# Attention row sums: from the exponentials' accumulator to adds of halves on GpSimd and a sum of 16 columns on VectorE

## The chip, the cores and the metric

The kernel runs on one core of a Trainium2 chip. The metric is the time of one execution on the device in microseconds (us). Five engines take their instructions each from a queue of its own, in order: TensorE (PE in the profile, its weight loads PEld), VectorE (DVE), ScalarE (ACT), GpSimd (POOL) and SyncE (SP, which issues most DMAs). They wait for each other by semaphores.

## The reference

Three stages follow one another: an attention with a window of 128 keys, a mixture of experts, and a feed-forward layer with squared ReLU. The change is in the attention:

```python
scores = scale * np.matmul(q, k.transpose(0, 1, 3, 2))      # 4 batches, 8 heads, 576 queries, head_dim 64
bias = slopes[:, None, None] * (-np.abs(rel))[None]
mask = (rel >= 0) & (rel < window)
scores = np.where(mask, scores + bias[None], -1000000000.0)
scores = scores - np.max(scores, axis=-1, keepdims=True)
attn = np.exp(scores)
attn = attn / (np.sum(attn, axis=-1, keepdims=True) + 1e-09)
return np.matmul(attn, v)
```

The sum in the line before the last is the row sum that the change computes in another way.

## The kernel before, in words

Each batch has five tiles of queries (t = 0 to 3 with 128 queries, t = 4 with 64). A unit is half of a tile's heads, `(b, t, hh)`; there are 40 units, 32 of them with t < 4. A query has 128 keys in its window; for a tile with t > 0 its 128 columns hold keys of two tiles, packed.

A loop over `k` runs the units through a hand-written pipeline; the order in which it calls the functions is the order of each engine's queue (no scheduler moves anything):

- `smax(units[k])` on DVE: packs the scores in PSUM (`copy_predicated`, L289), adds the bias, takes the minimum `m` per row (L294), four times per unit.
- `sexp(units[k], 0)` and, later in the same pass, `sexp(units[k], 1)` on ACT: two exponentials each (L315, 128 x 128, tile `e`); the accumulator output of each is one column of `rinv`, the row sum of one head. Units with t = 4 use L317.
- `sc(units[k + 1])` on PE: scores of the next unit.
- `tr(units[k - 2])` on PE turns `e`, `ev(units[k - 2])` copies it out of PSUM on ACT (`pt`, L344, L347, L350) and masks it on POOL with two selects (L354, L355); tiles with t = 0 have no selects.
- `background()` runs, one step at a time, the pieces of finished tiles (`post`) and of the routing (`route`, small operations on DVE, and three more pieces for the experts).
- `pv(units[k - 3])` on PE: probabilities times values, into `x`.

`post(u)`, after the second unit of a tile: first step, ACT copies `x` to `row` (L394); second step, one pass later, PE turns it and makes the router's logits (L403, into `m` and `x`), and DVE makes 1/sum: add 1e-9 (L405), reciprocal (L406); third step, DVE multiplies by it out of PSUM (L418, four instructions) and sums the logits (L419). A unit of t = 4 is normed on ACT ahead of `tr` (L329).

The attention ends at about 143 us. Behind it come the experts and the feed-forward layer, in which PE is busy nearly throughout (L743).

Of the kernel before, what the change touches and what calls it, by code (L numbers as in the profile page):

```python
# [8 lines left out]
F32 = mybir.dt.float32  # L9
# [3 lines left out]
AF = mybir.ActivationFunctionType  # L13
ALU = mybir.AluOpType
AX = mybir.AxisListType
# [3 lines left out]
B, H, S, D = 4, 8, 576, 64  # L19
# [34 lines left out]
def attention_moe_kernel(ctx, tc, qh, kh, v, mid, wg, mb, w1, w2, win, wout, out):  # L54
    nc = tc.nc
    dve, act, pe, pool = nc.vector, nc.scalar, nc.tensor, nc.gpsimd
# [4 lines left out]
    sm = ctx.enter_context(tc.tile_pool(name="sm", bufs=4))  # L61
# [72 lines left out]
    wk = ap("wk", 2)  # L134
# [6 lines left out]
    bias = ct([128, 2, H, 128], "bias", p=cst)  # L141
# [10 lines left out]
    rinv, st, pvb = {}, {}, {}  # L152
# [149 lines left out]
    def sexp(u, i):  # L302
        b, t, hh = u
        x, m = st[u]
        if i == 0:
            ex[u] = wk.tile([128, 2, 2, 128], F32, tag="e", name="e", bufs=3)
            if t == 4:
                rinv[u] = sm.tile([128, 2], F32, tag="rt", name="rt")
            elif hh == 0:
                rinv[b, t] = sm.tile([128, H], F32, tag="ri", name="ri")  # L310
        e = ex[u]
        if t < 4:
            for j in range(2):
                h = 4 * hh + 2 * i + j
                act.activation(e[:, i, j, :], x[:, i, j, :], AF.Exp, bias=m[:, i, j:j + 1], scale=-1.0, accum_out=rinv[b, t][:, h:h + 1])  # L315
        else:
            act.activation(e[:, i, 0, :], x[:, i, 0, :], AF.Exp, bias=m[:, i, 0:1], scale=-1.0, accum_out=rinv[u][:, i:i + 1])  # L317
        if i:
            st[u] = ex.pop(u)

    def norm_sums(u):
        r = rinv[u]
# [16 lines left out]
    def ev(u):  # L339
        b, t, hh = u  # L340
        p = st[u].rearrange("p (i j) q -> p i j q", i=2)
        st[u] = o = wk.tile([128, 2, 2, 2, 128], F32, tag="pt", name="pt")
        if t == 0:
            act.copy(o[:, :, 1], p)  # L344
            return
        if t == 4:
            act.copy(o[:, :, 0, 0, :], p[:, :, 0, :])  # L347
            prev, diag = (o[:n, :, k_, 0, :].rearrange("p i (j q) -> p i j q", j=2) for k_, n in ((0, 128), (1, 64)))
        else:
            act.copy(o[:, :, 0], p)  # L350
            prev, diag = o[:, :, 0], o[:, :, 1]
        n = 128 if t < 4 else 64
        kw = dict(base=0, fill=0.0)
        pool.affine_select(out=diag, in_=prev[:diag.shape[0]], pattern=[[0, 2], [0, 2], [1, n]], channel_multiplier=-1, compare_op=ALU.is_ge, **kw)  # L354
        pool.affine_select(out=prev, in_=prev, pattern=[[0, 2], [0, 2], [-1, n]], channel_multiplier=1, compare_op=ALU.is_gt, **kw)  # L355
# [31 lines left out]
    def post(u):  # L387
        b, t, _ = u
        g = group(u)
        if t < 4 or b % 2 == 0:  # L390
            xus[g] = row().rearrange("p (a b) -> p a b", a=4)
        xu = xus[g]
        c = slice(64 * (b % 2), 64 * (b % 2) + 64) if t == 4 else slice(0, 128)
        act.copy(xu[:, :, c], W0[:, :, c])  # L394
        if t == 4 and b % 2 == 0:
            return
        del xus[g]
        yield

        C = 128 + 2 * E  # L400
        xp = bank("m")[:, :3 * C].rearrange("p (a c) -> p a c", a=3), W0[:, 2:4, :].rearrange("p a b -> p (a b)")[:, None, :C]
        for i in range(4):
            pe.matmul(xp[i // 3][:, i % 3, :], xu[:, i, :], turned[:, i, :], start=True, stop=True)  # L403
        if t < 4:
            dve.tensor_scalar(rinv[b, t], rinv[b, t], 1e-9, None, op0=ALU.add)  # L405
            dve.reciprocal(rinv[b, t], rinv[b, t])  # L406
        yield
        xs = row()
        ls = sm.tile([128, H, E], F32, tag="ls", name="ls", bufs=2)
        r = rinv.pop((b, t)) if t < 4 else None  # L410
        for p, h0, n in ((xp[0], 0, 6), (xp[1], 6, 2)):
            hs = slice(h0, h0 + n)
            for o, w, d in ((xs.rearrange("p (h d) -> p h d", h=H)[:, hs, :], p[:, :, :128], D), (ls[:, hs, :], p[:, :, 128:], E)):
                o, w = o.rearrange("p (a j) d -> p a j d", j=2), w.rearrange("p a (j d) -> p a j d", j=2)
                if t == 4:
                    dve.tensor_copy(o, w)
                else:
                    dve.tensor_tensor(o, w, r[:, hs].rearrange("p (a j) -> p a j", j=2)[:, :, :, None].to_broadcast([128, n // 2, 2, d]), op=ALU.mult)  # L418
        dve.tensor_reduce(l_all[:, g, :], ls.rearrange("p h e -> p e h"), axis=AX.X, op=ALU.add)  # L419
        nc.sync.dma_start(out=xd[row_of(g):row_of(g) + 128, :], in_=xs)  # L420
        if g in gends:
            ready.append(route(g + 1 - gends[g], gends[g]))
# [226 lines left out]
    units = [(b, t, hh) for b in range(B) for t in range(5) for hh in range(2)]  # L649
# [321 lines left out]
    n = len(units)  # L971
# [26 lines left out]
    for k in range(n + 3):  # L998
        now, last = k < n, 0 <= k - 2 < n
        if now:  # L1000
            smax(units[k], 0)
            smax(units[k], 1)
        ended = 0 <= k - 1 < n and units[k - 1][1] == 4
        if ended:
            norm_sums(units[k - 1])
        if now:
            sexp(units[k], 0)
        if k + 1 < n:
            sc(units[k + 1])
            if k == 0:  # L1010
                keep_warm(WARM)
        if last:
            tr(units[k - 2])
            ev(units[k - 2])
        if now:
            sexp(units[k], 1)
        if ended:
            norm(units[k - 1])
        background()
        if k >= 3:  # L1020
            pv(units[k - 3])
        tail[0] = k
        background()
        tail[0] = 0
        if k % 2 == 0:
            for ahead, load in ((5, load_qk), (4, load_v)):
                if k // 2 + ahead < len(tiles):
                    load(*tiles[k // 2 + ahead])
        for at, make in ((0, gate_weights), (1, tail_bias), (2, route_loads), (5, logit_bias), (15, dump_rows)):
            if k == at:  # L1030
                make()
        if k >= FIRST_UP and primed:
            for _ in range(PIECES):
                next(first, None)
                background()
# [65 lines left out]
    for s in range(NSLOT):  # L1101
        n, nn = ({NSLOT - 1: SHORT, NSLOT - 2: MIDDLE}.get(i, SLOT) for i in (s, s + 1))
# [26 lines left out]
        if s == 2:  # L1129
            p = bank("v", (128, E))  # L1130
# [35 lines left out]
    p = ps = None  # L1166
# [10 lines left out]
    with tc.For_i(4 * (NSLOT - 1), total, 1) as ci:  # L1177
        e = nc.sync.value_load(le[0:1, bass.ds(ci, 1)], min_val=0, max_val=E - 1)
        o = pool.value_load(lo[0:1, bass.ds(ci, 1)], min_val=0, max_val=E * NCH - 1)
# [4 lines left out]
        for g in range(2):  # L1184
            r, p = row(), bank("v", (128, 4, 128))
# [337 lines left out]
```

## Time and profile before

| | us |
|---|---|
| median of 3 executions | 755.37 (754.91 to 756.37) |
| the profiled execution, its own time | 757.94 |
| its span, first to last instruction | 756.1 |
| PE busy in the span | 725.4 (96%) |
| DVE busy | 499.8 (66%) |
| ACT busy | 344.4 (46%) |
| POOL busy | 302.9 (40%) |

The profile was taken of one execution; the sums of the prediction are made against its own time, 757.94 us, which is 2.57 us above the median. The durations of one instruction are from this execution. An instruction's duration can overlap the start of the next one on its engine, so the step from start to start is shorter than the duration.

### The profile page before, as it was taken

Reading aid. Unit: us, or ns where it says so; the run is one execution under the profiler, and the core shown is the slowest. Engines: PE = TensorE matmul, PEld = TensorE weight load, DVE = VectorE, ACT = ScalarE, POOL = GpSimd, SP = SyncE. Lnnn points to the kernel's source line nnn. Section 1 sums busy time; section 2 is a strip of 40 time slices with the busy share of each in tenths; the row PEclk is TensorE's granted clock in tenths of the full one; section 3 lists DMA queues with packets and bytes.
Section 4 is the critical chain, followed back from the end, with each engine's and each line's share of the span. In section 5 each row is a group of like instructions: output and inputs, shape, how many; then the busy total and the mean of one; then the engine's idle time right before and its main releaser. Section 6 shows DMA issues by size and latency. Waiting matters only on the chain.

```text
span 756.1 us, 13418 instructions
## 1 busy us (share of the span) xinstructions
PE 725.4 (96%) x4567; PEld 627.3 (83%) x4567; DVE 499.8 (66%) x1288; ACT 344.4 (46%) x839; POOL 302.9 (40%) x328
## 2 busy tenths in 40 slices
PE   7899889999999999998989999999999999999997
PEld 6777757777788889887878898989989889899896
DVE  7788877779976967776464664466754768442542
ACT  6676658424534545454555565423324234231230
POOL 4322345303454434536162464425534246240431
PEclk9999999999999999999999999999999999999999
DMA  8558450139488685960679671879719796295832
GB/s 268 187 178 279 136 199 32 58 126 360 153 323 273 231 288 181 380 236 16 236 251 367 258 320 57 341 291 394 280 72 360 281 410 242 83 360 202 329 112 84
DMA packets 71110, 174.57 MB, mean 231 GB/s; under 512 B 10032, under 2 KB 18480, under 8 KB 71040
## 3 DMA queue, kind: packets, MB, share of 16 engines
q1 hardware_dynamic: 68048, 163.93, 59.7%
q0 software_dynamic: 2992, 9.77, 3.3%
q8 instruction: 37, 0.61, 0.3%
q14 instruction: 33, 0.27, 0.1%
HBM read 117.76 MB, written 55.90 MB: 230 GB/s over the span
## 4 chain that ended last, share of the span: by engine, by line
PE 48%; DMA 3%; DVE 1%; ACT 0%; issue 0%; ACTq 0%; SPq 0%
PE v L743 17%; PE s L743 12%; PE t L743 12%; PE x L743 3%; PE m L743 3%; DMA w<-yd 2%; DMA yd<-row,idx 1%; DVE cr L1314 1%; DVE cr L1339 0%; DVE xq L1258 0%; PE s L1355 0%; ACT hd L1306 0%; PE s L1423 0%; DVE row L1375 0%; ACT xq L1254 0%
## 5 line engine op out<-in xcount | busy, mean ns | idle before, releaser
L1307 POOL TENSOR_TENSOR hd<-cr,hd 128x384 fp32r<-128x384 f32 x96 | 113.1, 1213 | 140.9 <-ACT hd L1306 140.9
L743 PE MATMUL v<-w,hd 128*128 128x512 f32 x576 | 137.1, 390 | 0.4 <-ACT w L1358 0.4
L743 PEld LDWEIGHTS v<-w,hd 128*128 128x128 f32 x576 | 107.8, 188 | 22.6 <-ACT w L1358 0.7
L743 PE MATMUL s<-xq,w 128*128 128x384 f32 x576 | 108.1, 335 | 0.7 <-DVE cr L1339 0.7
L743 PEld LDWEIGHTS s<-xq,w 128*128 128x128 f32 x576 | 100.9, 188 | 2.1 <-issue 1.0
L743 PE MATMUL t<-w,h 128*128 128x512 f32 (+1 forms) x408 | 98.8, 395 | 2.1 <-DVE w L1213 2.1
L694 POOL TENSOR_TENSOR row<-row 128x512 int32<-128x512 int32 x32 | 45.5, 1421 | 129.7 <-DVE row L693 86.3
L743 PEld LDWEIGHTS t<-w,h 128*128 128x128 f32 (+1 forms) x408 | 73.4, 183 | 19.7 <-issue 2.6
L1306 ACT CAST hd<-cr 128x384 fp32r<-128x384 f32 x96 | 49.3, 514 | 66.4 <-DVE cr L1314 63.4
L743 PE MATMUL t<-w,hd 128*128 128x512 f32 x288 | 69.2, 389 | 0.0
L743 PE MATMUL s<-w 128*128 128x512 f32 (+2 forms) x292 | 66.2, 378 | 1.1 <-DVE h L768 1.1
L1375 DVE SCALAR_TENSOR_TENSOR row<-v,gate,row 128x512 f32<-128x512 f32 x36 | 27.0, 750 | 56.6 <-PE v L743 54.4
L315 ACT ACTIVATE e<-x,m 128x128 f32<-128x128 f32 x128 | 50.4, 398 | 30.0 <-DVE m L294 30.0
L743 PEld LDWEIGHTS t<-w,hd 128*128 128x128 f32 x288 | 54.1, 188 | 11.2
L672 DVE TENSOR_TENSOR w<-w 128x1024 fp32r<-128x1024 f32 x37 | 51.1, 1387 | 17.6 <-ACT w L669 15.5
L743 PEld LDWEIGHTS s<-w 128*128 128x128 f32 x292 | 53.2, 188 | 9.5 <-DVE h L768 2.0
L1336 ACT COPY cr<-s 128x384 f32<-128x384 f32 x48 | 23.0, 481 | 73.7 <-PE s L743 73.5
L1314 DVE SCALAR_TENSOR_TENSOR cr<-cr 128x384 f32<-128x384 f32 x72 | 52.5, 729 | 2.5
L354 POOL TENSOR_SCALAR_AFFINE_SELECT pt<-pt 128x512 f32<-128x512 f32 (+1 forms) x32 | 18.7, 586 | 75.0 <-ACT pt L350 58.7
L669 ACT CAST w<-w 128x1024 fp32r<-128x1024 f32 (+1 forms) x43 | 41.9, 990 | 2.0 <-DMA w<-w 2.0
L1339 DVE TENSOR_TENSOR cr<-t,cr 128x384 f32<-128x384 f32 x24 | 13.3, 554 | 44.1 <-PE t L743 44.1
L686 ACT ACTIVATE row<-w 128x512 f32<-128x512 f32 x32 | 21.3, 672 | 29.2 <-POOL row L694 25.6
(323 smaller groups left out, 1434.7 us busy)
## 6 DMA issues: line engine op xcount, KB each, us to landing
xq<-xs SPq DMA_DIRECT2D x42, 768.0 KB
w<-w SPq DMA_DIRECT2D x40, 512.0 KB, 5.4
xs<-xq SPq DMA_DIRECT2D x21, 768.0 KB, 3.4
ya<-row SPq DMA_DIRECT2D x54, 256.0 KB, 2.1
row<-ya SPq DMA_DIRECT2D x54, 256.0 KB, 8.8
w<-win SPq DMA_DIRECT2D x16, 512.0 KB, 7.2
wc<-row SPq DMA_DIRECT2D x32, 256.0 KB, 3.4
w<-wout SPq DMA_DIRECT2D x16, 512.0 KB, 5.2
```

The lines of the kernel that those rows point to most:

```text
L315: act.activation(e[:, i, j, :], x[:, i, j, :], AF.Exp, bias=m[:, i, j:j + 1], scale=-1.0, accum_out=rinv[b, t][:, h:h + 1])
L354: pool.affine_select(out=diag, in_=prev[:diag.shape[0]], pattern=[[0, 2], [0, 2], [1, n]], channel_multiplier=-1, compare_op=ALU.is_ge, **kw)
L669: act.copy(h[:, c], r[:, c])
L672: (eng or dve).tensor_tensor(l[:, c], r[:, c], h[:, c].bitcast(F32), op=ALU.subtract)
L686: act.mul(f, hi.bitcast(F32), 2.0 ** -112)
L694: pool.tensor_tensor(a, a, r, op=ALU.add)
L743: pe.matmul(ps, l, r, start=first and i == 0, stop=last and i == n - 1, **kw)
L1306: act.copy(gh, c)
L1307: pool.tensor_tensor(gl, c, gh.bitcast(F32), op=ALU.subtract)
L1314: dve.scalar_tensor_tensor(c, c, 0.0, c, op0=ALU.max, op1=ALU.mult)
L1336: act.copy(c, ps[q])
L1375: dve.scalar_tensor_tensor(o, ps, gate, o, op0=ALU.mult, op1=ALU.add)
```

## The change

The 128 exponentials of the units with t < 4 no longer have an accumulator output. A new function `part_sums` adds the two halves of the 128 columns, three times, on POOL: four heads at once, 4 x 64, 4 x 32 and 4 x 16 elements per partition. Its last output is a part of a new tile `ri` of 8 x 16 columns. In the second step of `post`, DVE sums the 16 columns of each head (a `tensor_reduce` of 8 x 16 to 8) ahead of the two instructions that were there. Units with t = 4 stay as they were. `part_sums` of unit k - 1 stands in the queue of POOL behind the selects of unit k - 2.

```diff
@@ sexp
             elif hh == 0:
-                rinv[b, t] = sm.tile([128, H], F32, tag="ri", name="ri")
+                rinv[b, t] = wk.tile([128, H, 16], F32, tag="ri", name="ri", bufs=4)
...
-                h = 4 * hh + 2 * i + j
-                act.activation(e[:, i, j, :], x[:, i, j, :], AF.Exp, bias=m[:, i, j:j + 1], scale=-1.0, accum_out=rinv[b, t][:, h:h + 1])
+                act.activation(e[:, i, j, :], x[:, i, j, :], AF.Exp, bias=m[:, i, j:j + 1], scale=-1.0)
...
+    def part_sums(u):
+        b, t, hh = u
+        s, n = st[u].rearrange("p i j k -> p (i j) k"), 128
+        while n > 16:
+            n //= 2
+            o = rinv[b, t][:, 4 * hh:4 * hh + 4] if n == 16 else wk.tile([128, 4, n], F32, tag=f"s{n}", name="s", bufs=1)
+            pool.tensor_tensor(o, s[:, :, :n], s[:, :, n:], op=ALU.add)
+            s = o
@@ post, second step
         if t < 4:
-            dve.tensor_scalar(rinv[b, t], rinv[b, t], 1e-9, None, op0=ALU.add)
-            dve.reciprocal(rinv[b, t], rinv[b, t])
+            r = sm.tile([128, H], F32, tag="ri", name="ri")
+            dve.tensor_reduce(r, rinv[b, t], axis=AX.X, op=ALU.add)
+            dve.tensor_scalar(r, r, 1e-9, None, op0=ALU.add)
+            dve.reciprocal(r, r)
+            rinv[b, t] = r
@@ the loop over k, behind tr and ev of unit k - 2
+        if 0 <= k - 1 < n and units[k - 1][1] < 4:
+            part_sums(units[k - 1])
```

On POOL, in the first batch, the queue before held only the selects, two for each unit (`pt` with the number of its buffer), each pair waiting for ACT's copy:

```order
L354 AFFINE_SELECT pt_465<-pt_465 128x2x256 [waits Activation_49]
L355 AFFINE_SELECT pt_465<-pt_465 128x2x256 [waits Pool_49]
L354 AFFINE_SELECT pt_511<-pt_511 128x2x256 [waits Activation_49]
L355 AFFINE_SELECT pt_511<-pt_511 128x2x256 [waits Pool_49]
L354 AFFINE_SELECT pt_576<-pt_576 128x2x256 [waits Activation_49]
L355 AFFINE_SELECT pt_576<-pt_576 128x2x256 [waits Pool_49]
```

The same units now, the selects under their new line numbers L362 and L363 (`e` holds the exponentials, `s` the halves, `ri` the 16 columns):

```order
L362 AFFINE_SELECT pt_480<-pt_480 128x2x256 [waits Activation_49]
L363 AFFINE_SELECT pt_480<-pt_480 128x2x256 [waits Pool_49]
L326 TENSOR_TENSOR s_484<-e_414 128x256
L326 TENSOR_TENSOR s_486<-s_484 128x128 [waits Pool_49]
L326 TENSOR_TENSOR ri_368<-s_486 128x64 [waits Pool_49]
L362 AFFINE_SELECT pt_531<-pt_531 128x2x256 [waits Activation_49]
L363 AFFINE_SELECT pt_531<-pt_531 128x2x256 [waits Pool_49]
L326 TENSOR_TENSOR s_535<-e_457 128x256
L326 TENSOR_TENSOR s_537<-s_535 128x128 [waits Pool_49]
L326 TENSOR_TENSOR ri_458<-s_537 128x64 [waits Pool_49]
L362 AFFINE_SELECT pt_603<-pt_603 128x2x256 [waits Activation_49]
L363 AFFINE_SELECT pt_603<-pt_603 128x2x256 [waits Pool_49]
```

Three adds, each waiting for the one before it, now stand between one unit's selects and the next unit's.

On DVE, the end of the first tile before (`m` and `x` in L418 are PE's products):

```order
L405 TENSOR_SCALAR ri_297<-ri_297 128x8
L406 RECIPROCAL ri_297<-ri_297 128x8 [waits DVE_49]
L418 TENSOR_TENSOR row_532<-m_517,ri_297 128x384 [waits DVE_49,PE_49]
L418 TENSOR_TENSOR ls_533<-m_517,ri_297 128x48
L418 TENSOR_TENSOR row_532<-x_191,ri_297 128x128 [waits PE_49,Activation_49]
```

And now, the same place:

```order
L414 TENSOR_REDUCE ri_547<-ri_297 128x8 [waits Pool_49]
L415 TENSOR_SCALAR ri_547<-ri_547 128x8 [waits DVE_49]
L416 RECIPROCAL ri_547<-ri_547 128x8 [waits DVE_49]
L429 TENSOR_TENSOR row_559<-m_542,ri_547 128x384 [waits DVE_49,PE_49]
L429 TENSOR_TENSOR ls_560<-m_542,ri_547 128x48
L429 TENSOR_TENSOR row_559<-x_191,ri_547 128x128 [waits PE_49,Activation_49]
```

One instruction is added per tile, ahead of the other two; it waits for POOL, and L415 waits for it. The queues of PE and SP hold the same instructions in the same order as before, and ACT's too, without the accumulator outputs.

## Rows read from the trace of the kernel before

**Rows 1.** Busy us (and instructions) of PE, PEld, DVE, ACT, POOL; granted clock, DMA.

```profile
120.00:140.00 20.00, 17.58 (x189) 14.22 (x188) 17.23 (x82) 14.58 (x51) 11.15 (x16) 1.00 0.20 67
```

**Rows 2.** Waits from 0 to 225 us: us in total, times, longest.

```profile
ACT e L315 <- DVE m L294: 30.0, 16, 3.8
...
DVE row L418 <- PE m L403: 7.7, 10, 2.8
...
DVE row L418 <- PE x L374: 5.3, 9, 0.7
```

**Rows 3.** ACT in order of time, one pass: start, us, what ran.

```profile
35.97 0.40 ACT L315 ACTIVATE e<-x,m 128x128 f32<-128x128 f32 x1
...
36.75 0.68 ACT L329 ACTIVATE e<-e,rt 128x128 f32<-128x128 f32 x2
37.34 0.57 ACT L394 COPY row<-x 128x512 f32<-128x512 f32 x1
```

**Rows 4.** PE in order of time, waits for ACT in brackets (idle us, releaser).

```profile
26.04 1.00 PE L403 MATMUL m<-turned,row 128*128 128x144 f32 x6 [0.90 <-ACT row L394]
...
37.20 0.62 PE L337 MATMUL v<-ident,e 128*128 128x128 f32 x2 [0.43 <-ACT e L329]
...
56.17 1.00 PE L403 MATMUL m<-turned,row 128*128 128x144 f32 x6 [0.19 <-ACT row L394]
...
67.67 0.62 PE L337 MATMUL v<-ident,e 128*128 128x128 f32 x2 [0.65 <-ACT e L329]
...
89.09 1.00 PE L403 MATMUL m<-turned,row 128*128 128x144 f32 x6 [0.90 <-ACT row L394]
...
102.59 0.62 PE L337 MATMUL v<-ident,e 128*128 128x128 f32 x2 [0.72 <-ACT e L329]
...
126.27 1.00 PE L403 MATMUL m<-turned,row 128*128 128x144 f32 x6 [0.34 <-ACT row L394]
```

**Rows 5.** DVE groups by shape, 0 to 225 us: busy us, mean ns.

```profile
L419 DVE TENSOR_REDUCE l_all<-ls 128x8 f32<-128x64 f32 x18 | 4.9, 271 | 0.6
...
L405 DVE TENSOR_SCALAR ri<-ri 128x8 f32<-128x8 f32 x16 | 4.8, 302 | 0.0
...
L479 DVE TENSOR_REDUCE row<-row 128x3 f32<-128x60 f32 x5 | 1.1, 217 | 0.2
...
L475 DVE TENSOR_REDUCE row<-row 128x3 f32<-128x24 f32 x5 | 0.9, 178 | 0.2
```

**Rows 6.** Line L405 alone: duration ns min/median/max.

```profile
L405 DVE TENSOR_SCALAR ri<-ri x16: 158/166/615, 16.2 to 141.1; 128x8 f32<-128x8 f32 x16
```

**Rows 7.** POOL groups by shape, 0 to 225 us.

```profile
L354 POOL TENSOR_SCALAR_AFFINE_SELECT pt<-pt 128x512 f32<-128x512 f32 x24 | 15.4, 641 | 58.8 <-ACT pt L350 58.7
...
L672 POOL TENSOR_TENSOR w<-w 128x512 fp32r<-128x512 f32 x6 | 7.5, 1278 | 4.7 <-ACT w L669 4.7
...
L355 POOL TENSOR_SCALAR_AFFINE_SELECT pt<-pt 128x256 f32<-128x256 f32 x8 | 3.4, 425 | 0.5
```

**Rows 8.** POOL in order of time, two units of the second batch, and the weights' split.

```profile
60.90 0.64 POOL L354 TENSOR_SCALAR_AFFINE_SELECT pt<-pt 128x512 f32<-128x512 f32 x1 [2.12 <-ACT pt L350]
61.61 0.64 POOL L355 TENSOR_SCALAR_AFFINE_SELECT pt<-pt 128x512 f32<-128x512 f32 x1
62.73 0.67 POOL L354 TENSOR_SCALAR_AFFINE_SELECT pt<-pt 128x512 f32<-128x512 f32 x1 [0.48 <-ACT pt L350]
...
138.55 2.53 POOL L672 TENSOR_TENSOR w<-w 128x512 fp32r<-128x512 f32 x2 [0.21 <-ACT w L669]
```

**Rows 9.** DVE in order of time at the same two moments.

```profile
62.80 0.61 DVE L405 TENSOR_SCALAR ri<-ri 128x8 f32<-128x8 f32 x1
...
138.38 2.78 DVE L493 TENSOR_SCALAR row<-iota,row 128x128 fp32r<-128x128 f32 x3
```

**Rows 10.** Line L493 alone on DVE: duration ns min/median/max.

```profile
L493 DVE TENSOR_SCALAR row<-iota,row x18: 338/342/1309, 47.7 to 160.0; 128x128 fp32r<-128x128 f32 x18
```

**Rows 11.** PE in order of time: probabilities times values of the second unit of Rows 8.

```profile
65.10 1.09 PE L374 MATMUL x<-pt,vS 128*64 128x128 f32 x16
```

## The prediction

> **What bounds the kernel now.** I read the busy times by stretch first, then the waits, then the order of time on each engine. The change touches only the attention, the first 143 us; behind it PE is the bound, so what the attention gains or loses arrives at the end one for one, unless a load is late, and none is issued in another order. Within the attention no engine is full [rows 1]: of the 20 us from 120 to 140, PE is busy for 17.6, DVE for 17.2, ACT for 14.6, POOL for 11.2. The reader is to see that ACT, which the change relieves, is the third of the four. The waits say the same [rows 2]: ACT waits for DVE's row minima 30.0 us in all, in 16 places. There a faster ACT only waits longer. But there is a loop through all of them, once per tile: DVE's minima start ACT's exponentials, behind these ACT copies the finished tile to `row`, PE turns it (L403), and DVE multiplies (L418), which it must do before the next unit's minima. DVE waits for PE's `m` there in 10 of 16 tiles, 7.7 us, and for `x` in 9, 5.3 us [rows 2]. In those tiles DVE has time to spare, and what ACT saves shortens the loop; in the others DVE runs without a pause and ACT's saving is lost.
>
> **What the change removes.** Two exponentials with accumulators take 36.75 - 35.97 = 0.78 us from start to start, two multiplications of the same shape without them 37.34 - 36.75 = 0.59 [rows 3]. So an accumulator costs 0.095 us, the four of a unit 0.38, the 128 of the kernel 12 us of ACT. How much is on the path is read from PE's waits for ACT that have a unit's four exponentials ahead of them. Seven of them count [rows 4]: 0.90, 0.43, 0.65, 0.90 and 0.72 are longer than the saving and give 0.38 each, 0.19 and 0.34 give themselves, in sum 2.4 us. A few more such waits stand where DVE has no idle time; I count them at zero. The bounds: nothing, if DVE always comes last, and 16 x 0.38 = 6.1 if each tile's loop gave the whole.
>
> **What it adds on DVE: 16 reductions.** The nearest row has half of the input and the same output, 271 ns (L419). Two others give the price of an element: from 24 to 60 of them, 178 to 217 ns, 1.1 ns each [rows 5]; 64 more make 0.34 us. It lies between 0.27 and twice that, 0.54. In the 10 tiles with a wait for `m` it is hidden by that wait; in 6 it is not: 6 x 0.34 = 2.0 us (0 if other pauses hide it; 16 x 0.54 = 8.6 if nothing does).
>
> **What it adds on POOL: 96 adds.** The trace has no add that small there. From a select of 512 to one of 256 elements, 641 to 425 ns, the fixed part is some 0.21 us; an add or subtraction of 512 takes 1.278 [rows 7], so 2.1 ns an element. Then 256, 128 and 64 elements cost 0.74, 0.48 and 0.34, 1.56 us per unit (1.12 in proportion to the elements alone; 3 x 1.278 = 3.8 if size didn't matter, which the selects speak against). Each waits for the one before it, which between two selects leaves 61.61 - 60.90 - 0.64 = 0.07 us [rows 8]. So a unit costs POOL 1.41 us for the selects, as before, and 1.77 for adds, 3.2 in all; the units follow each other every 3.5 us on average (L405 runs from 16.2 to 141.1 us, 18 tiles of two units [rows 6]). Over the 32 units the adds are 50 us of work on an engine that had room for them, but only just.
>
> First consequence: **selects come late**. In the second batch two units follow closely: selects from 60.90, then from 62.73 [rows 8]. With adds between them the second pair starts at 60.90 + 1.41 + 1.77 = 64.1 and ends 1.35 later, at 65.4; PE wants it at 65.10 [rows 11]. That is 0.3 us late, more where POOL was late already. There is one such place in each of four batches, and PE's wait behind it (0.65 us in this one [rows 4]) takes part of it back. I take 1.0 us in all; the bounds are 0, with adds of 1.12 us, and 32 x 1.9 = 61 with adds that size doesn't shorten (1.41 + 3.8 + 0.21 = 5.4 us per unit), an end I hold for all but excluded.
>
> Second consequence: **POOL holds up DVE**. At 62.80 DVE's L405 takes 0.61 us, and ends when the select that began at 62.73 does [rows 8, 9]; unhindered it takes 0.158 [rows 6]. At 138.38 three instructions of L493 take 2.78 us instead of some 0.85 (0.34 each [rows 10], overlapping), beside two subtractions on POOL that take 2.53 [rows 8, 9]. [...]
>
> The rows alone would allow two readings. If only instructions that meet an add by chance are held up, the price goes by POOL's work, as below. If the adds, which begin just behind the selects, meet L405 in every tile, that line loses 16 x (0.61 - 0.158) = 7.2 us instead of 2.3, and the sum is higher by some 3 us.
>
> The price per us of POOL's work: L405 loses 16 x (0.302 - 0.158) = 2.3 us [rows 5, 6] to 37.6 us of selects (two of each group, 15.4 and 3.4 [rows 7]), 0.06 us per us. That is one line; the routing's small operations with two inputs are hit too, so I take 0.09: 50 x 0.09 = 4.5 us of DVE. The subtractions beside L493 give the other end, 1.93 / 2.53 = 0.76 per us where DVE has nothing else to run, 38 us; the adds stand beside `smax` and L418, which read PSUM, for most of their time, so I stay near the low end. Half of the 4.5 falls where DVE waits for PE anyway [rows 2]: 2.2 us on the path, between 0 and some 8 for twice the rate with nothing absorbed.
>
> **The sum.** -2.4 + 2.0 + 1.0 + 2.2 = +2.8 us on the profiled execution's 757.94. This stood 2.57 above the median of 755.37, so the median becomes 758.2 us. What ACT and SP do otherwise costs nothing: the three buffers of `e` now also wait for POOL's first add of the unit three before, which is queued two passes ahead, some 6 us; the cover is gone only if POOL falls two units behind.
>
> **The rivals.** A measurement of this kernel can tell about 0.2%, 1.5 us, from no change.
>
> - *Faster: ACT's relief passes through the loop.* For it: PE's waits for ACT in rows 4, and DVE's 13.0 us of waits in L418. Then the 2.4 us come (3.5 with the waits that I left out), the reductions fall into DVE's waits, and DVE is blocked only there: 755.37 - 2.9 = 752.5. It decides if DVE's extra time per tile stays below its waits for `m` and `x`, 13.0 / 16 = 0.8 us, in most tiles. Against it: six tiles have no wait for `m`.
> - *No measurable change.* The gain of 2.4 is real and the losses are half as large: 755.4. The point is a loss of DVE of some 2 us.
> - *POOL becomes the bound.* If an add of a dependent chain costs a fixed 0.45 instead of 0.21 us, a unit takes 3.9 us of POOL, and the 24 units with selects run over the 3.5 by 0.4 each, 9.6 us less some pauses: some 763. For it: POOL has 11.15 of 20 us already near the end [rows 1]. Against it: eight units without selects and eight of t = 4 let it catch up.
> [...]
>
> **How the numbers follow.** Chances: the forecast, a loss of 1.5 to 5 us, 0.36; faster 0.23; no measurable change 0.22; POOL the bound 0.10; blocking 0.09. So faster 0.23, same 0.22, slower 0.55. The likeliest case alone has 757 to 760.5. The range leaves out a tenth at either end: below, the better half of the faster case, at 753.0; above, the worse parts of the last two, at 762.5.
>
> **What would show it.** In the profile after: ACT's group of exponentials loses the accumulator reads, its step falls from 0.39 to 0.30, and its waits for DVE grow from 30 us towards 40. POOL's adds take 0.74, 0.48 and 0.34. PE's waits for `row` shrink where rows 4 count them. DVE's L415 has a mean above L405's 302 ns, and small operations of the routing show maxima near an add's duration. The reductions take 0.34 us and DVE doesn't wait for POOL at them. Selects behind adds wait on nothing but POOL, and PE waits for the selects once per batch. The prediction is wrong if DVE's idle time before L418 takes up all of the reductions and blocking, or if POOL is 95% busy from 20 to 140 us.

## The result, and the profile after

The changed kernel takes 765.22 us (762.03 to 766.67, 4 runs) beside 755.73 us before: ratio 1.0121, interval 1.0102 to 1.0140. It is slower, as forecast, but by 9.5 us instead of 2.8, and outside the range (753.0 to 762.5). The profiled execution took 766.67 us, with a span of 765.0.

First the groups by shape of the kernel after, which answer to [rows 5] and [rows 7] (line, engine, operation, tiles, shapes; busy us, mean ns; idle time of the engine before, and who ended it):

```profile
L314 ACT ACTIVATE e<-x,m 128x128 f32<-128x128 f32 x128 | 44.0, 397 | 45.4 <-DVE m L294 45.4
L326 POOL TENSOR_TENSOR s<-e 128x256 f32<-128x256 f32 x32 | 23.3, 727 | 2.9 <-ACT e L314 2.9
L326 POOL TENSOR_TENSOR s<-s 128x128 f32<-128x128 f32 x32 | 14.6, 457 | 2.5
L326 POOL TENSOR_TENSOR ri<-s 128x64 f32<-128x64 f32 x32 | 10.6, 330 | 2.5
...
L415 DVE TENSOR_SCALAR ri<-ri 128x8 f32<-128x8 f32 x16 | 5.2, 324 | 0.6
...
L414 DVE TENSOR_REDUCE ri<-ri 128x8 f32<-128x128 f32 x16 | 4.4, 276 | 0.0
```

The adds and the reductions have about the forecast lengths, and no reduction waited for POOL. ACT's idle time behind DVE's minima is 45.4 us, where [rows 2] have 30.0. That is not only ACT's doing: in the runs below it is 34.4 us where ACT is faster and nothing is added, and 37.7 us where adds stand on POOL beside the old ACT. The rest is in the order of time. PE's long pauses in the attention (start, us, what ran; idle before it and who ended it):

```profile
12.14 0.51 PE L268 MATMUL s<-kS,qS 64*64 64x192 f32 x2 [2.29 <-DVE m L294]
...
25.56 0.89 PE L274 MATMUL s<-kS,qS 128*128 128x192 f32 x4 [1.71 <-issue]
...
81.50 0.38 PE L480 MATMUL v<-row,upper 128*128 128x16 f32 x1 [2.11 <-DVE t_acc L519]
...
101.21 1.27 PE L411 MATMUL m<-turned,row 128*128 128x144 f32 x6 [2.01 <-ACT e L337]
...
125.63 1.76 PE L382 MATMUL x<-pt,vS 128*64 128x128 f32 x14 [2.64 <-POOL pt L363]
...
145.09 1.09 PE L382 MATMUL x<-pt,vS 128*64 128x128 f32 x16 [1.85 <-POOL pt L363]
```

And stretches of the same execution: busy us (and instructions) of PE, PEld, DVE, ACT and POOL, then the granted clock, the share of its full clock that TensorE was given, and DMA:

```profile
80.00:85.00 5.00, 3.50 (x36) 2.82 (x37) 4.21 (x27) 2.93 (x8) 2.74 (x5) 0.63 0.62 213
85.00:90.00 5.00, 5.00 (x55) 4.38 (x54) 2.52 (x13) 1.18 (x3) 2.75 (x5) 0.69 0.00 0
100.00:105.00 5.00, 3.79 (x26) 3.22 (x28) 2.54 (x13) 1.16 (x5) 1.90 (x4) 0.67 0.02 8
120.00:125.00 5.00, 2.24 (x28) 1.61 (x20) 3.91 (x17) 3.34 (x11) 4.75 (x8) 1.00 0.31 94
125.00:130.00 5.00, 4.37 (x47) 3.65 (x47) 2.25 (x14) 0.62 (x2) 4.62 (x9) 0.66 0.14 52
120.00:140.00 20.00, 15.37 (x161) 12.54 (x153) 14.80 (x75) 11.52 (x34) 17.92 (x29) 0.91 0.15 51
```

Two things are to be seen. POOL, 11.15 us busy from 120 to 140 us in [rows 1], is now busy for 17.92, and PE waits there for the selects. And behind four of these six pauses (12, 81, 101, 125 us; not 25 and 145) PE runs for 3 to 7 us at a granted clock of 0.50, half of the 1.00 before and after (read in windows of 1 us); windows that hold part of such a stretch show a clock between, 0.63 to 0.91 in these rows. The kernel before has one such stretch, too, in its profiled execution:

```profile
110.00:115.00 5.00, 3.64 (x31) 2.52 (x33) 3.93 (x26) 3.57 (x16) 0.95 (x1) 0.68 0.73 289
```

POOL in the place of the fourth pause (119 to 126 us, kernel after):

```profile
119.20 0.95 POOL L727 DMA_INDIRECT row<-xd,idx  x1 [0.30 <-issue]
120.17 0.74 POOL L326 TENSOR_TENSOR s<-e 128x256 f32<-128x256 f32 x1
120.98 0.45 POOL L326 TENSOR_TENSOR s<-s 128x128 f32<-128x128 f32 x1
121.51 0.32 POOL L326 TENSOR_TENSOR ri<-s 128x64 f32<-128x64 f32 x1
121.79 2.49 POOL L683 TENSOR_TENSOR w<-w 128x512 fp32r<-128x512 f32 x2
124.23 0.64 POOL L362 TENSOR_SCALAR_AFFINE_SELECT pt<-pt 128x512 f32<-128x512 f32 x1
124.94 0.64 POOL L363 TENSOR_SCALAR_AFFINE_SELECT pt<-pt 128x512 f32<-128x512 f32 x1
```

A gather for the first expert, three adds, a weight split of 2.49 us, and only then the selects that PE waits for until 125.63. Nearly all of the loss is made in the attention: the first product of the experts (L743, L754) starts at 146.1 us instead of 137.6, the last 9.0 us later.

**Lag.** To follow the loss I use DVE's first multiplication of each tile (L418 before, L429 after) and subtract its start in the profiled execution before. Since that one has its half-clock stretch between tiles (2,3) and (3,0), a kernel without a stretch there gains about 2 us in that step; the row of the kernel before with fills, one of the runs below (from 32 to 144 us it has no stretch: 16 products of L374 take 1.09 us throughout), shows the level, 1.71, and the kernel after gains 2.39. In us, at the last tile of batches 1 and 2 and at three tiles of batch 3 (tiles are named by batch and t, the runs are explained below):

| profiled execution of | (1,3) | (2,3) | (3,0) | (3,1) | (3,3) |
|---|---|---|---|---|---|
| before, with fills | -0.30 | -0.27 | -1.98 | -2.25 | -1.47 |
| after | +1.19 | +5.72 | +3.33 | +6.58 | +8.24 |
| after again | +0.54 | +1.58 | -0.80 | +3.60 | +5.25 |
| after, two pauses filled | +0.29 | +1.31 | -1.09 | +1.84 | +3.44 |
| no sums (ones) | -1.93 | -2.70 | -1.86 | -0.20 | +1.05 |
| fixed sums | -1.12 | -1.88 | -3.32 | -1.66 | +0.69 |
| reductions, no adds | -0.78 | -1.45 | -2.84 | -0.03 | +1.51 |
| adds beside accumulators | +4.16 | +8.07 | +5.82 | +9.42 | +10.55 |
| change in batches 0 to 2 | -0.24 | +1.14 | +0.90 | +0.88 | +0.90 |
| change in batch 3 only | -0.42 | -0.80 | -3.16 | +0.08 | +2.16 |
| all but tile (3,0) | +0.60 | +1.97 | +1.56 | +3.24 | +4.80 |
| fixed sums, accumulators in batch 3 | -1.98 | -1.28 | -2.99 | -3.59 | -1.96 |

### The profile page after: what moved, and what is told of

Same layout as the page of the kernel before. It is cut to its first block, busy times and chain, and to the rows that moved or that the text cites. A ratio compares the mean times of both kernels' runs of the same rounds, so it can differ in the third digit from the quotient of the medians.

```text
span 765.0 us, 13408 instructions
## 1 busy us (share of the span) xinstructions
PE 731.3 (96%) x4567; PEld 633.4 (83%) x4567; DVE 509.4 (67%) x1304; ACT 333.0 (44%) x711; POOL 349.8 (46%) x424
## 4 chain that ended last, share of the span: by engine, by line
PE 48%; DMA 2%; DVE 2%; ACT 0%; issue 0%; SPq 0%; POOLq 0%; POOL 0%
PE v L754 17%; PE t L754 12%; PE s L754 12%; PE x L754 3%; PE m L754 3%; DMA w<-yd 1%; DVE cr L1327 1%; DMA yd<-row,idx 0%; DVE cr L1352 0%; DVE xq L1271 0%; PE s L1368 0%; ACT hd L1319 0%; SPq L1105 0%; DVE row L1388 0%; ACT xq L1267 0%
## 5 line engine op out<-in xcount | busy, mean ns | idle before, releaser
L754 PE MATMUL v<-w,hd 128*128 128x512 f32 x576 | 137.1, 390 | 0.4 <-ACT w L1371 0.4
L754 PEld LDWEIGHTS v<-w,hd 128*128 128x128 f32 x576 | 107.8, 188 | 22.9 <-ACT w L1371 0.9
L754 PE MATMUL s<-xq,w 128*128 128x384 f32 x576 | 108.1, 335 | 0.7 <-DVE cr L1352 0.7
L705 POOL TENSOR_TENSOR row<-row 128x512 int32<-128x512 int32 x32 | 45.4, 1419 | 129.6 <-DVE row L704 86.4
L754 PEld LDWEIGHTS s<-xq,w 128*128 128x128 f32 x576 | 100.9, 188 | 2.1 <-issue 1.0
L754 PE MATMUL t<-w,h 128*128 128x512 f32 (+1 forms) x408 | 100.4, 400 | 2.1 <-DVE w L1226 2.1
L754 PEld LDWEIGHTS t<-w,h 128*128 128x128 f32 (+1 forms) x408 | 74.6, 186 | 20.2 <-issue 2.6
L754 PE MATMUL t<-w,hd 128*128 128x512 f32 x288 | 69.2, 389 | 0.0
L754 PE MATMUL s<-w 128*128 128x512 f32 (+2 forms) x292 | 66.2, 378 | 1.2 <-DVE h L779 1.2
L314 ACT ACTIVATE e<-x,m 128x128 f32<-128x128 f32 x128 | 44.0, 397 | 45.4 <-DVE m L294 45.4
L754 PEld LDWEIGHTS t<-w,hd 128*128 128x128 f32 x288 | 54.1, 188 | 11.2
L754 PEld LDWEIGHTS s<-w 128*128 128x128 f32 x292 | 53.2, 188 | 9.6 <-DVE h L779 2.0
L382 PE MATMUL x<-pt,vS 128*64 128x128 f32 x448 | 34.5, 297 | 5.0 <-POOL pt L363 4.7
L382 PEld LDWEIGHTS x<-pt,vS 128*64 128x64 f32 x448 | 26.2, 147 | 10.3 <-POOL pt L363 5.7
```

The source lines that it names most:

```text
L382: pe.matmul(W0[64 * j:64 * j + 64, hp, :], vS[b][:, k_, 64 * h:64 * h + 64], o[:, i, k_ - t + 1, j, :], start=n == 0, stop=n == len(kb) - ...
L705: pool.tensor_tensor(a, a, r, op=ALU.add)
L754: pe.matmul(ps, l, r, start=first and i == 0, stop=last and i == n - 1, **kw)
```

## The experiments

Eighteen runs, one of them the kernel after again, in five sets on four chips. The kernel before, which ran beside them in each set, had medians of 755.8 to 759.4 us; so ratios are compared, each with the kernel before of the same set. Behind a ratio stands its 95% interval.

**The change taken apart.** Adds alone, with the accumulators kept (the row sums of the adds go to a tile that nobody reads):

```diff
-pool.tensor_tensor(rinv[b, t][:, 4 * hh:4 * hh + 4], ...)
+pool.tensor_tensor(part[b, t][:, 4 * hh:4 * hh + 4], ...)   # exponentials as before
```

> The kernel before, accumulators and all, with the 96 adds on POOL writing to a tile that nobody reads; no reductions. It gives what the adds cost by sitting on POOL, with nothing gained and no one waiting for their results. If the adds are the whole loss (POOL's queue late, DVE held up, PE slowed behind its waits), the time is 755.7 + 9.5 + 2.4 = about 767, or 765 if there was no gain on ACT to lose. If the loss of the after kernel comes from the chain add, reduction, reciprocal instead, the time is near 756.

Measured: 767.73 us, 1.0106 (1.0080 to 1.0132). The adds alone cost as much as the whole change. PE waits for the selects here too, though ACT has its old pace:

```profile
128.03 1.34 PE L387 MATMUL x<-pt,vS 128*64 128x128 f32 x10 [1.91 <-POOL pt L368]
```

DVE has the same instructions as before here, so they can be compared one by one: summed over the attention and the routing they take some 7 us more (some 172 before). 23 instructions that stand beside an add make 6.3 us of it, and what others gain and lose beside selects and splits of weights that now fall elsewhere nearly cancels. L197 grows from 2.2 to 3.9 us, the line that answers to L405 from 4.8 to 6.2. One of its instructions (DVE and POOL in order of time; the second add of three):

```profile
54.09 0.46 DVE L418 TENSOR_SCALAR ri<-ri 128x8 f32<-128x8 f32 x1
...
54.06 0.45 POOL L331 TENSOR_TENSOR s<-s 128x128 f32<-128x128 f32 x1
```

It ends when the add does, at 54.55 beside 54.51 us. The longest, 1.252 us, stands beside a split of weights, not beside an add. The run isn't the whole change without ACT's saving in every respect: ACT waits 5.0 us for POOL's adds here, which read `e`, and in the kernel after it doesn't.

ACT's saving alone, without adds and reductions:

```diff
-part_sums(units[k - 1])
-dve.tensor_reduce(r, rinv[b, t], axis=AX.X, op=ALU.add)
-dve.tensor_scalar(r, r, 1e-9, None, op0=ALU.add)
+dve.tensor_scalar(r, fixed, 1e-9, None, op0=ALU.add)   # fixed: a constant tile
```

> The exponentials have no accumulators, and nothing sums: the adds and the 16 reductions are left out, and the division uses ones. What is left is ACT's saving alone. If the saving passes through the loop as the prediction has it (2.4 us), the time is about 753.3 us against 755.7 before, and ACT's waits for DVE grow from 30 us by about 12. If it is lost entirely in ACT's waits, 755.7. If the after kernel is slow because ACT is now early and something else meets badly, this one is slow too: over 760.

> No accumulators, no adds, no reductions; the division uses one fixed number per head, close to its row sums, so that the router sends the tokens to the same experts in nearly the same numbers and the whole time can be compared. What is left is ACT's saving alone. By the prediction 2.4 us faster than before, 0.997. If ACT's saving disappears in its waits for DVE, as the attention of the run without sums suggests (its end came 1.0 us later, not earlier), 1.000 within 0.002.

The one with ones instead of the sums sent tokens to other experts, and its later stages grew (1499 us); only its attention can be read. With fixed numbers near the sums: 761.02 us, 1.0020 (1.0008 to 1.0032). No gain is left. But the table of lags shows that there was one: -1.9 to -2.7 us at the end of batch 2, as forecast, and batch 3 takes it back.

Reductions without adds, from a constant tile:

```diff
-dve.tensor_reduce(r, rinv[b, t], axis=AX.X, op=ALU.add)
+dve.tensor_reduce(r, fixed, axis=AX.X, op=ALU.add)
```

> As the run without sums, but with the 16 reductions of 8 x 16 on DVE, which read a constant tile; the adds are left out. If a reduction of 0.28 us is exposed in 6 tiles, it is 1.7 us above the run without sums, some 755; if DVE's waits hide it, no difference; if each is on the path, 4.5 us above.

Its later stages grew as well (943 us). In the attention it stands 1.25 us behind the one with ones at the end of batch 2, after 12 of 16 reductions.

**Where the loss is.** The same edit with a condition:

```diff
-act.activation(e[:, i, j, :], x[:, i, j, :], AF.Exp, ...)
+kw = {} if cond else dict(accum_out=rinv[b, t][:, h:h + 1])
+act.activation(e[:, i, j, :], x[:, i, j, :], AF.Exp, ..., **kw)
```

with `b < 2`, `b >= 2`, `b < 3`, `b == 3`, `(b, t) != (3, 0)` and `t > 0`; adds and reductions go with it.

> The change in batches 0 and 1 only; batches 2 and 3 keep the accumulators. If POOL's shortage beside gathers and weight splits in batches 2 and 3, with PE's clock behind its waits, is the cause, the loss is what the lag shows up to 72 us, about 1.5 us: 757. If DVE is held up by the adds wherever they run, half of the loss is here: about 760.5.

> The change in batches 2 and 3 only. The whole change costs 1.2%, the first half alone 0.4%. If POOL's shortage beside gathers and splits, with PE's waits and half clock behind them, is the main loss, this half costs 0.7 to 1.0%, 5 to 7.5 us. If the loss goes by the number of adds, as in the rival that DVE is held up, it costs the same as the first half, 0.4 to 0.6%.

> The change in batches 0 to 2 only; batch 3 keeps the accumulators. Between the first and the second tile of batch 3 the changed kernel loses 3 to 5 us in each trace. If that is POOL's queue in that one batch (gathers, splits and adds together, PE waiting 2.6 us for the selects), leaving the change out there gives 4 to 6 us back: ratio 1.004 to 1.007. If every add costs alike, a quarter of the loss: 1.009 to 1.012.

> The counterpart: the change in batch 3 only. POOL's queue in that batch as the cause: 1.006 to 1.008, with PE's wait of some 2.6 us for the selects of the first unit with t = 1. Every add alike: 1.003 to 1.004.

> The change everywhere but in one tile, t = 0 of batch 3, whose two units' adds stand on POOL between the gathers and the weight split; those two keep their accumulators. Six of 96 adds (3.1 us of POOL) go. If the order on POOL is the cause, the selects of the next unit come some 3 us earlier, PE's wait of 2.6 us shrinks to under 0.5, and 2 to 4 us come back: 1.008 to 1.012, beside 1.012 to 1.016 for the whole change. If not, no more than 6 parts in 96 of the loss, 0.6 us.

> The change everywhere but in the four tiles with t = 0, which keep their accumulators: no adds beside DVE's start of the kernel (the eight instructions of the tail bias took 3.16 us instead of 2.26 beside adds, and PE paused 2.2 us there) and none between the gathers and the split. A quarter of the adds goes. By their places 4 to 6 us come back, 1.005 to 1.009; by their number a quarter, 1.009 to 1.012.

| change in | ratio | interval |
|---|---|---|
| batches 0 and 1 | 1.0039 | 1.0016 to 1.0062 |
| batches 2 and 3 | 1.0063 | 1.0043 to 1.0083 |
| batches 0 to 2 | 1.0048 | 1.0026 to 1.0070 |
| batch 3 | 1.0059 | 1.0045 to 1.0073 |
| all but tile (3,0) | 1.0098 | 1.0077 to 1.0119 |
| all but t = 0 | 1.0114 | 1.0096 to 1.0131 |
| everything | 1.0121 | 1.0102 to 1.0140 |
| everything, again | 1.0158 | 1.0135 to 1.0181 |

The two halves fell between what was expected of either reading and decide nothing. Batch 3, with a quarter of the adds, costs as much as the other three together (the intervals overlap), and leaving it out came out as expected of POOL's queue, not of adds that cost alike. With the change in batch 3 only, PE's waits for the selects are there:

```profile
119.15 1.09 PE L384 MATMUL x<-pt,vS 128*64 128x128 f32 x16 [2.41 <-POOL pt L365]
...
138.58 1.09 PE L384 MATMUL x<-pt,vS 128*64 128x128 f32 x16 [1.84 <-POOL pt L365]
```

In the table of lags, from (3,0) to (3,1) every kernel that has the adds in batch 3, or lacks the accumulators there, loses 1.7 to 4.4 us (adds beside accumulators 3.6), and the two that have the accumulators without adds there, and before with fills, lose nothing. Leaving out the six adds of tile (3,0) removes PE's wait for the selects at that place. But of the 9.5 or 11.6 us of the whole change only some 2 to 5 come back, and against the first of its two results, 1.0121, the intervals overlap, since another pause takes its place (PE in order of time, all but tile (3,0)):

```profile
134.71 0.28 PE L484 MATMUL v<-row,upper 128*128 128x24 f32 x1 [3.14 <-ACT pt L360]
```

Leaving out the adds of all four tiles with t = 0 was no better, 1.0114 where 1.005 to 1.009 was expected by their places (and 1.009 to 1.012 by their number): that pause of 3.14 us is there, too, and the start, which it relieves (lag -0.26 at the first tile, +0.86 in the kernel after), is a small part.

**What the other pause is.** At the same place the run with fixed sums, which has no adds at all, pauses as well. DVE, POOL, ACT and PE of that run, in order of time:

```profile
124.53 1.94 DVE L471 TENSOR_TENSOR cum<-cum,row 128x8 fp32r<-128x8 f32 x3
...
125.18 2.50 POOL L682 TENSOR_TENSOR w<-w 128x512 fp32r<-128x512 f32 x2
...
128.77 0.40 ACT L316 ACTIVATE e<-x,m 128x128 f32<-128x128 f32 x1 [2.48 <-DVE m L296]
...
129.79 0.39 PE L479 MATMUL v<-row,upper 128*128 128x24 f32 x1 [3.09 <-ACT pt L358]
```

The same instructions in the kernel before:

```profile
127.10 0.57 DVE L461 TENSOR_TENSOR cum<-cum,row 128x8 fp32r<-128x8 f32 x3
...
128.86 2.50 POOL L672 TENSOR_TENSOR w<-w 128x512 fp32r<-128x512 f32 x2
...
130.43 0.40 ACT L317 ACTIVATE e<-x,m 128x128 f32<-128x128 f32 x1 [0.61 <-DVE m L296]
...
131.45 0.28 PE L469 MATMUL v<-row,upper 128*128 128x24 f32 x1 [1.23 <-ACT pt L350]
```

Before, the split begins 1.76 us behind the start of DVE's three additions; with a faster ACT, whose copy of `pt` releases the selects ahead of the split, 0.65 us behind. It meets them, they take 1.94 instead of 0.57 us, DVE's next minima are late, ACT waits 2.48 us for them instead of 0.61, its copy of `pt` stands behind, and PE waits 3.09 us for the copy instead of 1.23. The additions aren't the whole of DVE's 1.66 us there: two other small instructions meet selects (0.57 and 0.55 us instead of 0.18 each), and the one that answers to L405, 0.61 us before, meets none and takes 0.16.

In the kernels without the adds of (3,0) or of t = 0 the additions are late in the same way, 1.39 and 1.40 us, but beside a select and an add. In the kernel after they take 0.67 us, and 0.57 in its second profile: there this collision doesn't happen, and PE's long pauses in batch 3 are those for the selects.

To test this, accumulators back in batch 3 of the run with fixed sums:

> As the run with fixed sums, but the last batch keeps its accumulators, and so ACT's pace; adds and reductions are left out. With fixed sums everywhere the lag was -3.3 us at the first tile of the last batch and +0.7 at its end. If ACT's saving in that batch is what brings the weight split on POOL forward onto DVE's three additions (1.94 us instead of 0.57) and with it PE's pause of 3.1 us, the lag stays near -2.5 to -3 and the time is 0.996 to 0.997. If the last batch takes the gain back for another reason, such as loads that come no earlier, 0.999 to 1.002 as with fixed sums everywhere.

Measured: 756.19 us, 1.0005 (0.9992 to 1.0018). The additions are short again and end before the split:

```profile
123.52 0.57 DVE L475 TENSOR_TENSOR cum<-cum,row 128x8 fp32r<-128x8 f32 x3
...
125.27 2.49 POOL L686 TENSOR_TENSOR w<-w 128x512 fp32r<-128x512 f32 x2
```

From (3,0) to (3,1) it loses nothing (-0.60), and PE's pause there is 1.51 us: ACT's pace in that batch brings the collision. But the time expected of it, 0.996 to 0.997, did not come; it lies in the range that was named for another reason (0.999 to 1.002), so that the collision is what costs the time isn't shown. The profiled execution is 1.0 to 1.5 us ahead of before with fills at (3,0) to (3,2), not 3, and 0.5 at (3,3); it has two half-clock stretches.

**Splits moved from POOL to DVE**, in the kernel after and in the kernel before, and the third one alone in the kernel before:

```diff
-wsplit(key, None, pool if s == 0 and j < 3 else None, ...)
+wsplit(key, None, None, ...)                        # the third alone: j < 2
```

> The kernel after, with the three splits of weights that stand between the adds and the selects in the last batch (two subtractions of 512 columns each) on DVE, one of 1024 columns, 1.4 us each. If selects that come late behind splits and adds cause PE's waits of 2.6 and 1.85 us, and the half clock after the first, 3 to 5 us of the 9.5 come back, less up to 3 us for DVE's new work: 762 to 764. If late selects aren't the cause, DVE's work only adds: 766 to 768.

> The kernel before, with the three weight splits of the last batch on DVE instead of POOL. It is the counterpart of the kernel after with the same move, 1.013. If that one's loss came of DVE's own new work (3 x 1.2 to 1.4 us in a batch in which DVE sets the pace), this one loses 3 to 5 us as well: 1.004 to 1.007. If it came of the adds that are still there, 1.000 to 1.002.

> The kernel before, with the third split alone on DVE. On POOL it holds up three of DVE's instructions at 138.38 us, 2.78 us instead of 0.85. If that collision is on the path, 1.9 us are saved and 1.2 to 1.4 spent: 0.999 to 1.000, a little faster than before. If DVE has time to spare there, 1.001 to 1.003.

Measured: 769.56 us, 1.0131 (1.0104 to 1.0158); 765.56 us, 1.0130 (1.0114 to 1.0146); 757.18 us, 1.0009 (0.9998 to 1.0021). The first says nothing for late selects: the move itself is as dear as the whole change. The second was expected at 1.004 to 1.007; what I missed is that on DVE the split waits in the queue for ACT's casts, and DVE's other work with it, 2.01, 2.45 and 1.05 us at the three splits (DVE, then PE, of the kernel before with its splits on DVE):

```profile
130.08 1.23 DVE L672 TENSOR_TENSOR w<-w 128x1024 fp32r<-128x1024 f32 x1 [2.45 <-ACT w L669]
...
135.54 0.39 PE L469 MATMUL v<-row,upper 128*128 128x24 f32 x1 [4.45 <-ACT pt L350]
```

It is the same chain a third time: something makes DVE late in batch 3, ACT's exponentials of t = 4 wait, the copy of `pt` behind them, and PE, 4.45 us where the kernel before has 1.23. The third split alone gains nothing: no version here is faster than the kernel before.

**The clock.** Matmuls whose result is overwritten or unread, where PE pauses:

```diff
+for _ in range({(3, 1, 0): 16, (3, 3, 1): 10}.get(u, 0)):     # in pv; first trial: 8 and 8
+    pe.matmul(W0[:, 2 * hh, :], ident, ident, start=True, stop=True)
+for _ in range({2: 12, 24: 13, 29: 12, 37: 7}.get(k, 0)):     # behind ev, in the loop over k
+    pe.matmul(W0[:, 3, 16:], ident, ident[:, 16:], start=True, stop=True)
```

> The kernel after, with eight matmuls of 128 columns, whose result is overwritten, ahead of the products with the values at the two places where PE waits 2.64 and 1.85 us for the selects: PE works, some 1.7 us, while it would wait. If the half clock at 125 to 130 us comes of PE's pause, the granted clock stays at 1.00 there, and 1.5 to 2.5 us come back: 763. If the clock falls for another reason, nothing comes back: 765, or up to 767 where the pauses are shorter in other runs.

> The kernel after, unchanged, beside the next three on one chip. If the half-clock stretches come and go from run to run, the profiled execution shows them at other places or not at all, and the times again go with the mean granted clock, some 4.8 us for each 0.01. Ratio 1.008 to 1.013. If the stretches belong to the program, they stand where they stood: at 13, 81, 101 and 125 us.

> The kernel after, with matmuls of 112 or 128 columns, whose result nobody reads, at the six places where PE pauses 1.1 to 2.6 us (before 12.1, 81.5, 101.2, 125.6, 138.1 and 145.1 us): PE works while it would wait. If the pauses bring the half clock, the mean clock rises from 0.990 to 0.995 or more, and 2 to 4 us come back against the unfilled kernel beside it. If the clock falls regardless, the mean clock stays, and the time with it, or it is longer by the matmuls that no longer fall into a pause, up to 3 us.

> The kernel before, with six or seven such matmuls at three of its pauses (before 79.8, 96.6 and 131.5 us). Its mean clock is 0.994, so if the pauses bring the half clock, up to 2 us are to be had: 0.998. If not, 1.000 to 1.002.

With two places filled: 764.12 us, 1.0078 (1.0054 to 1.0102); no run of the kernel after stands beside it. In its profile the clock is 1.00 from 120 to 130 us, and a stretch follows another pause, 2.29 us before 133.31. The kernel after, again: 767.35 us, 1.0158, more than the 1.008 to 1.013 expected; in its profile the stretches at the first pause and at the first wait for the selects are there again (from 11.5 and 121 us), and those at 81 and 101 us aren't, though it pauses 2.11 and 2.03 us at the same two places. With six places filled, in the same set: 765.87 us, 1.0126 (1.0108 to 1.0144), mean clock 0.994 to 1.000 in its six executions, 0.9975 on average, where the unfilled kernel has 0.984 to 0.991 in five. Its profiled execution has no stretch below 1.00; two of its windows:

```profile
85.00:90.00 5.00, 4.97 (x72) 4.07 (x72) 4.83 (x27) 1.83 (x6) 3.48 (x7) 1.00 0.14 50
...
125.00:130.00 5.00, 5.00 (x73) 4.21 (x69) 3.87 (x20) 2.32 (x8) 4.18 (x9) 1.00 0.14 52
```

So the pauses bring most of the half clock: where PE works through them, the lowest clock of six executions, 0.994, is above the highest of five unfilled ones, 0.991. The time is less certain. The fills cost PE nearly what they give back; 1.5 us of 11.6 came back, and the two intervals overlap. In the kernel before they cost more than they gave, 758.86 us, 1.0034 (1.0016 to 1.0051); on that chip it had a mean clock of 0.998 already, so that there was little to get back. A pause doesn't always bring the half clock: the run with two fills is the same program as the kernel after up to batch 3, pauses 2.11 us at the same place (80.58 us), and keeps its clock:

```profile
80.00:85.00 5.00, 4.42 (x66) 3.74 (x70) 4.35 (x25) 3.97 (x11) 3.72 (x7) 1.00 0.47 162
85.00:90.00 5.00, 3.88 (x53) 3.02 (x53) 4.89 (x27) 2.23 (x6) 3.01 (x6) 1.00 0.51 162
```

Between these two executions the lag differs by 4.4 us at (2,3), 5.72 and 1.31: that is what the three stretches at 13, 81 and 101 us cost together, if nothing else differs.

A straight line through the times of all kernels over their mean clock, one level for each kernel and for each set of the kernel after, gives 4.8 us for each 0.01 (standard error 0.2). The two runs with longer later stages are left out, and one execution of the kernel before with fills, which has a mean clock of 0.947 and is no slower for it (760.07 us). At one clock, 0.998, the kernel before comes to 756.7, the kernel after to 761.0 and 761.9, adds beside accumulators to 762.7, fixed sums to 757.0. So 4.3 to 5.2 us of the loss come at the same clock, and the rest, some 5 to 6 us, by the clock, which the pauses bring. This is a fit, not an experiment, and it hangs on what is left out: with that one execution the slope is 2.3, and the loss at one clock 5.7 to 7.4 us. The run with six fills bears it out in direction.

## Why the prediction was wrong

Three steps failed: selects that come late were put at 1.0 us and cost PE 4.7; ACT's saving was counted as gained or lost, and in batch 3 it can turn against the kernel; and the sum had no term for the granted clock. One by one:

**ACT's saving, -2.4 us.** Right to the end of batch 2 (-1.9 and -2.7 us without sums) and wrong for the whole: the run with fixed sums gained nothing. The step that failed is "in the others DVE runs without a pause and ACT's saving is lost". With nothing added, in batch 3 it isn't lost, it turns against the kernel: ACT's copies come earlier, POOL's selects and split behind them move onto DVE's small instructions, and PE pauses 3.09 us instead of 1.23. I had costed what ACT does otherwise at nothing. In the kernel after itself the late selects stand in the place of this collision.

**Reductions, +2.0 us.** 276 ns instead of 340, and 1.25 us after 12 of them. About right.

**The length of the adds.** 0.727, 0.457 and 0.330 us measured, 0.74, 0.48 and 0.34 forecast. The rival that a dependent add has a fixed cost of 0.45 us fell.

**POOL holds up DVE.** 4.5 us of DVE forecast, some 5 measured in the kernel after (the same instructions before and after, without the reductions), some 7 with adds beside accumulators. In the kernel after, 18 instructions that stand beside adds make 4.4 us of it. Right in direction, a little low; how much of it is on the path, forecast at 2.2, no run shows. Others pay than the line that I had counted: L415 is held up to 871 and 955 ns beside splits of weights and 566 beside a select, and at the four places where it meets an add first it takes 171 to 183 ns. The new reduction stays between 267 and 282 ns in all 16 places, 14 of them beside work of POOL. The low rate took it that `smax` and L418 aren't held up and that small operations of the routing are, and the trace of the kernel before has both: L294 takes 268 to 293 ns in all its 128 instructions of 128 x 128, 49 of them beside work of POOL, and the widest product of L418 541 to 559 in all 16, 15 of them beside such work, while L453 takes 658 ns beside a select at 93.83 us, where its median is 182. That reading PSUM is the reason, no run shows. Blocking has 0.09 in the chances and a part in the upper end of the range, 762.5; that it is the main cost, at the 8 us of twice the rate, no run shows either. What the runs showed in its place are the 5 and 7 us of DVE above, on the path or not.

**Selects come late, +1.0 us.** This is the term that was mis-sized. I looked for closely following units in each of four batches and found one of 0.3 us. POOL wasn't short there; it was short in batch 3, where the gathers stand in the same queue, which I had not in view, and the splits, which I had in view only as a price per element and as something that holds up DVE. PE waits 4.7 us for the selects in all, 2.64 and 1.85 of them in batch 3, and with the change in that batch alone 2.41 and 1.84. "One of four batches" should have been read as four unlike batches: [rows 1] showed the 11.15 us of POOL in the last one, and eight units with 1.6 us of adds each fall into that batch, five of them into that window. The rival that POOL is the bound named the right engine and nearly the right time, 763, for a wrong reason, and its sign, 95% busy from 20 to 140 us, isn't there: 57 to 74% up to 120 us, 90% behind.

**Not in the sum: the granted clock.** The forecast took each pause at its own length. Up to the end of batch 2 the executions with no stretch, or only the one at 11 to 14 us, lag by 1.3 and 1.6 us; the forecast's terms for that part (six of the seven waits, 2.1 us, and three quarters of the rest, 3.9) sum to 1.8. With three stretches the same program lags 5.7 us. So the sum was right up to the end of batch 2 where the clock held, and the two things missing are batch 3 and the clock. That its terms came out there one by one is shown for ACT's saving and the reductions only.

What stays open: which pauses bring the lower clock and which don't. The same pause of 2.11 us did both. Also not shown is how the loss at the same clock divides between late selects, DVE's instructions held up and DVE's chain in batch 3, since each takes the other's place when it is removed.

## What to carry to other kernels

Cost added work on a shared engine in the stretch where that engine is fullest, not by a mean over equal-looking batches: a quarter of the adds, alone, cost as much as the other three quarters (1.0059 and 1.0048). A faster engine also releases others' work earlier, so look at what it will start and whom that will meet: with fixed sums ACT's saving, a lag of -1.88 us at the end of batch 2, was gone within one batch (+0.69 at its last tile). And a pause of TensorE can cost more than its length: behind four of the six pauses of 1.71 to 2.64 us in the kernel after it went on for 3 to 7 us at a granted clock of 0.50, and three such stretches made 4.4 us between two executions, if nothing else differed. Sum such pauses with that in mind, and compare executions by their mean clock before explaining a difference of 1%.

## What the runs showed that was not expected

The time goes with the mean granted clock, 4.8 us for each 0.01 by the fit above, and that clock differs from one set to another for one and the same program: the kernel before has 0.998 on average in two sets (755.8 and 756.4 us) and 0.994 in three others (758.5 to 759.4 us). It isn't the chip alone, since one of the chips had both, 758.9 us in the first set and 756.4 in the last. Moving three subtractions of 1.2 us from POOL to DVE, 3.7 us of work, cost the kernel before 1.3%, as much as the 96 adds. In its profile they bring DVE's queue waits for ACT of up to 2.45 us and PE a pause of 4.45 us, with 7 us at a granted clock of 0.50 behind it.
